# Loading and normalising a small probability table in four parts in place of one

## Chip, cores and metric
The kernel runs on one core of a Trainium2 chip. The metric is the device time of one execution in microseconds (us), median of several runs. The engines are named as in the profile: PE (TensorE), PEld (its weight loads), DVE (VectorE), ACT (ScalarE), POOL (GpSimd), and SP (SyncE), which in this kernel issues all but two of the DMAs, in the order of the program.

## The reference
A linear attention feeds a mixture of four experts. The 2304 tokens of the second stage stand in 18 tiles of 128.

```python
# attention: batch 4, heads 8, sequence 576, head size 64, 128 features
def phi(x):
    proj = np.einsum('bhsd,df->bhsf', x, w_phi)
    proj = proj - np.max(np.abs(proj), axis=-1, keepdims=True)
    return np.concatenate([np.exp(proj), np.exp(-proj)], axis=-1)
q_p, k_p = (phi(q), phi(k))
kv = np.einsum('bhsf,bhsd->bhfd', k_p, v)
num = np.einsum('bhsf,bhfd->bhsd', q_p, kv)
den = np.einsum('bhsf,bhf->bhs', q_p, np.sum(k_p, axis=2))[..., None] + 1e-06
attn_out = num / den
# mixture of experts: x is attn_out as (2304, 512), E = 4, F = 1024
p = domain_probs / (domain_probs.sum(-1, keepdims=True) + 1e-9)
for e in range(E):
    h = np.maximum(x @ w1[e], 0.0)
    out += p[:, e:e + 1] * (h @ w2[e])
```

`domain_probs` is the small table of this case: 2304 rows of 4 numbers of 32 bits.

## The kernel before
The 16 pairs of heads of the attention are worked on one after the other, a new one every 16 "steps" of a clock that exists only while the program is written. Each stage of a pair (load, projection `proj`, its row maxima `m` and the subtraction `d`, exponentials, the product `kv`, the numerator `num`, the denominator's reciprocal `rec`, storing) has a step in a table, and `later(key, fn)` puts it on a heap. `run_until` takes from the heap what is due. From the fourth pair on the experts run in the gaps: `first_units` works through all four experts for the first four token tiles (4 tiles of 128, tiles 0 to 3), and calls `tick()` after every few matmuls, which moves the clock on and issues what is due of the attention. The other 14 tiles follow when the attention is over, in two groups that use Strassen products. So the order of each engine's instructions is set by these keys, and every engine works through its own list in order.

Names that the text uses: `l2` (shown as `l`) is the PSUM tile of an expert's second layer, 128x512. Its pool `ps_l2` has two buffers while the attention runs. DVE frees one by the eviction at line 753, `out = l * pr + out`, which reads the normalised probability `pr` of the tile and expert. `proj` and `num` tiles take turns in `ps_att`, which has three buffers; a `proj` buffer is free when DVE's subtraction at line 333 (`d`) has read it. POOL makes the low parts of numbers that PE multiplies in two pieces: `elo` (line 359), `w1lo` and `w2lo` (line 651), `klo` and `qs` (line 244), each a subtraction of two SBUF tiles. At line 217 DVE casts `qs`, and POOL's subtraction of line 244 on `qs` needs that cast. `mt` and `mb` belong to the query's maxima: `mt` is written to DRAM and read back as a broadcast `mb` (line 297), which DVE subtracts at line 302.

The table is loaded in one DMA at step 38 into `pr` (128 partitions, 18 tiles, 4 experts), and `probs_norm` normalises it at step 46 with four DVE instructions: sums, plus 1e-9, reciprocal, product.

Of the kernel before, what the change touches and what calls it, by code (L numbers as in the profile page):

```python
# [14 lines left out]
ALU = mybir.AluOpType  # L15
AX = mybir.AxisListType
# [4 lines left out]
def kernel(  # L21
# [16 lines left out]
    nc = tc.nc  # L38
    P = 128
# [5 lines left out]
    NE, NFC = w.shape[0], w.shape[1]  # L45
    DM = NP * P
    NTT = NT // P
    NPAIR = B * NP

    N0, N1 = 4, 4  # L50
# [42 lines left out]
    pr = const.tile([P, NTT, NE], F32, name="pr")  # L93
    prs = const.tile([P, NTT], F32, name="prs")
# [22 lines left out]
    def later(key, fn):  # L117
        heapq.heappush(queue, (key, next(count), fn))

    def run_until(key):  # L120
        while queue and queue[0][0] <= key:
            heapq.heappop(queue)[2]()
# [661 lines left out]
    def first_units():  # L784
        pend = []
        for n in range(NU):
            load("w1", n + 2, W_WAIT[0])
            h_hi = hp_.tile([P, 2, 512], F32R, name="h_hi", tag="h_hi")
            h_lo = hp_.tile([P, 2, 512], F32R, name="h_lo", tag="h_lo")
            for f in range(2):  # L790
                for k in range(NP):
                    l1_part(n, f, k)
                    if k < NP - 1:
                        tick()
                ps = banks.pop((n, f))
                nc.scalar.activation(h_hi[:, f], ps, AF.Relu)
                relu_lo(h_lo[:, f], ps, h_hi[:, f])
                tick()
            l1_done(n, W_WAIT[2:])
            if n:  # L800
                load("w2", n + 1, W_WAIT[1])
            for fn in pend:
                fn()
                tick()
            if pend:
                l2_done(n - 1, W_WAIT[2:])
            pend = [
                functools.partial(l2_tile, n, (h_hi, h_lo), j, j, out0[:, j]) for j in range(N0)
            ]
        return pend  # L810
# [8 lines left out]
    def x_load(x, first, nt, wait=0):  # L819
        raw = x.raw = early[0].tile([P, NP, 512], F32, name="xr", tag="xr", bufs=1)  # L820
        a = first * P
        src = xd[:, :, a : a + nt].rearrange("c p t -> p c t")
        after(wait, lambda: nc.sync.dma_start(raw[:, :, :nt], src))
# [49 lines left out]
    def spread(ops, start, gap):  # L873
        for i, fn in enumerate(ops):
            after(start + gap * i, fn)
# [93 lines left out]
    def second_units(pend):  # L969
        xs, ops = xa, None  # L970
        for n in range(NU, 3 * NU):
            hooks = {}
            if n == 2 * NU:
                xs = xb
            if n == 2 * NU - 1:
                ops["t4"] = ops["T1"] + ops["t4"]
                for i, name, start, gap in (
                    (1, "T2", 0.5, 0.5), (2, "t4", 0.5, 1), (4, "T3", 0.5, 1.2),
                    (5, "B22", 0.5, 2.3), (6, "T4", -2, 2.1),
                ):  # L980
                    hooks[i] = functools.partial(spread, ops[name], start, gap)
            if n == 2 * NU - 2:
                ops = x_ops(xb)
                spread(ops["t"] + ops["t3"], 0.4, 1.3)
            if n == NU + 3:
                x_load(xb, xb.first, xb.nt)
                for k in range(NP):
                    after(4 + k, nc.scalar.activation, x0_hi[:, k, : xb.nt], xb.raw[:, k, : xb.nt], AF.Copy)
                    after(
                        6 + k,  # L990
                        lambda k=k: nc.vector.tensor_tensor(
                            x0_lo[:, k, : xb.nt], xb.raw[:, k, : xb.nt],
                            x0_hi[:, k, : xb.nt].bitcast(F32), op=ALU.subtract,
                        ),
                    )
            if n == NU + 6:
                x_load(xb, xb.first + xb.nt // P, xb.nt)
            h = strassen_unit(n, xs, pend, hooks)
            nj = xs.nt // P
            pend = [  # L1000
                functools.partial(
                    l2_tile, n, h[b], j, xs.first + b * nj + j, (out0 if b == 0 else out1[0])[:, j]
                )
                for b in (1, 0) for j in range(nj)
            ]
        for fn in pend:
            fn()
            tick()


    with tc.manual_schedule():
        nc.vector.memset(wbd, 0.0)
        nc.scalar.dma_start(wbd[0:D, 0:NF], w_phi)
        nc.scalar.dma_start(wbd[D:P, NF : 2 * NF], w_phi)
        nc.vector.memset(out0[:, 0, 0:256], 0.0)
        warm = ps_l2.tile([P, 512], F32, name="warm", tag="l2")
        for _ in range(3):
            nc.tensor.matmul(
                warm[:, 0:256], lhsT=out0[:, 0, 0:P], rhs=out0[:, 0, 0:256], start=True, stop=True
            )  # L1020
        run_until(-25)
        make_identity(nc, ident)
        nc.vector.memset(eps, 0.0)
        nc.vector.memset(eps[64:P, 0:1], 1e-6)
        nc.vector.memset(eps[0:64, 1:2], 1e-6)
        for h in range(2):
            r = slice(h * D, (h + 1) * D)
            nc.vector.tensor_copy(wst[r], wbd[r, h * NF : (h + 1) * NF])
        nc.vector.tensor_copy(wst_hi, wst)
        nc.vector.tensor_tensor(wst_lo, wst, wst_hi.bitcast(F32), op=ALU.subtract)  # L1030
        nc.gpsimd.tensor_tensor(wlo0[0:64], wst[0:64], wst_hi[0:64].bitcast(F32), op=ALU.subtract)
        zero = wst_hi[64:P].bitcast(F32)
        nc.gpsimd.tensor_tensor(wlo0[64:P], zero, zero, op=ALU.subtract)
        nc.vector.tensor_copy(wbd_hi, wbd)
        nc.vector.tensor_tensor(wbd_lo, wbd, wbd_hi.bitcast(F32), op=ALU.subtract)
        later(38, lambda: nc.sync.dma_start(pr, probs.rearrange("(t p) e -> p t e", p=P)))

        def probs_norm():
            nc.vector.reduce_sum(prs, pr, axis=AX.X)
            nc.vector.tensor_scalar_add(prs, prs, 1e-9)  # L1040
            nc.vector.reciprocal(prs, prs)
            nc.vector.tensor_tensor(
                pr, pr, prs.unsqueeze(2).to_broadcast([P, NTT, NE]), op=ALU.mult
            )

        later(46, probs_norm)
        for n in range(2):
            for i, kind in enumerate(("w1", "w2")):
                for o, fn in ((0, w_load), (8, w_hi), (11.5, w_lo)):
                    later(FETCH[2 * n + i] + o, functools.partial(fn, kind, n))  # L1050
        run_until(FIRST)
        xa, xb = Pair(), Pair()
        xa.first, xa.nt = N0, 512
        xb.first, xb.nt = N0 + 8, 384
        for x, hi, lo in ((xa, x1_hi, x1_lo), (xb, x0_hi, x0_lo)):
            x.op = {
                "B11": (hi[:, 0:2, : x.nt], lo[:, 0:2, : x.nt]),
                "B21": (hi[:, 2:4, : x.nt], lo[:, 2:4, : x.nt]),
            }
        out1 = []  # L1060

        xa_ops = {}

        def to_early():

            in_stack.close()
            early.append(
                ctx.enter_context(
                    tc.tile_pool(name="early", bufs=1, side="right", reuse_waits="tile")
                )  # L1070
            )
            x_load(xa, xa.first + 4, xa.nt)
            xa_ops.update(x_ops(xa))
            fns = [fn for k in ("t", "T2", "T1", "t3", "T3") for fn in xa_ops[k]]
            for i, fn in enumerate(fns):
                later(LAST_IN + X_IN + X_GAP * i, fn)

        def to_late():

            att_stack.close()  # L1080
            late.append(ctx.enter_context(tc.tile_pool(name="late", bufs=1, reuse_waits="tile")))
            out1.append(late[0].tile([P, 4, DM], F32, name="out1"))

        later(LAST_IN, to_early)
        later(LAST + XA_LATE, to_late)
        clock.key = FIRST
        clock.step = (LAST - FIRST) / (NU * (2 * NP + 2 * N0) * SPREAD)
        pend = first_units()
        clock.key = max(clock.key, LAST + XA_LATE)
        run_until(clock.key)  # L1090
        clock.step = 1
        spread([fn for k in ("B22", "t4", "T4") for fn in xa_ops[k]], XA_START, XA_GAP)
        second_units(pend)
# [38 lines left out]
```

## Time and profile before
| what | value |
|---|---|
| median of 3 runs | 942.47 us (941.11 to 943.03) |
| profiled execution | 941.14 us |
| its span, first to last instruction | 939.0 us |
| PE busy | 930.8 us (99%) |
| DVE busy | 648.1 us (69%) |
| POOL busy | 530.3 us (56%) |
| ACT busy | 439.3 us (47%) |
[...]

The profiled execution is one run; its span leaves out 2.1 us of the device time that the runs count. Shares are averages over stages that differ: the attention ends at about a third of the span, and the four places of this case lie in that third.

### The profile page before, as it was taken

To read this page: it belongs to the slowest core of one execution; us is meant where nothing else is said; L and a number is where in the kernel's file an instruction comes from. 1 tells how busy PE (TensorE), PEld (TensorE's weight loads), DVE (VectorE), ACT (ScalarE), POOL (GpSimd) and SP (SyncE) were. 2 spreads that over 40 slices of the span, in tenths; PEclk is the share of its full clock that TensorE was granted. 3 is DMA by queue.
4 is the path that set the end of the run, shared out by engine and by line. 5 is a ranking of instruction groups with operands and counts; after the bars stand their busy time and mean duration, and the time that the engine had idled before them with its cause. 6 is when DMAs were issued, how large, how long until landed. Compare 5 with 4: busy or idle time off the path is not lost.

```text
span 939.0 us, 13221 instructions
## 1 busy us (share of the span) xinstructions
PE 930.8 (99%) x4834; PEld 810.3 (86%) x4834; DVE 648.1 (69%) x1040; ACT 439.3 (47%) x788; POOL 530.3 (56%) x376
## 2 busy tenths in 40 slices
PE   9999999999999999999999999999999999999998
PEld 8988888888888887888888888888899898989897
DVE  6876888878878689566665555669856565656555
ACT  5676666667666545333333333334524343434331
POOL 5646767757556477544445544444765656565651
PEclk9999999999999999999999999999999999999999
DMA  6644555555653633321211221111151212121201
GB/s 164 147 117 137 149 154 144 148 170 152 170 151 99 193 97 112 88 82 45 79 45 45 71 65 45 45 45 46 45 173 51 91 45 90 45 90 45 90 23 68
DMA packets 77418, 90.70 MB, mean 97 GB/s; under 512 B 38410, under 2 KB 40202, under 8 KB 77354
## 3 DMA queue, kind: packets, MB, share of 16 engines
q1 hardware_dynamic: 77194, 89.80, 32.5%
q8 instruction: 38, 0.62, 0.3%
q14 instruction: 26, 0.21, 0.1%
q10 hardware_dynamic: 160, 0.07, 0.0%
HBM read 81.94 MB, written 7.90 MB: 96 GB/s over the span
## 4 chain that ended last, share of the span: by engine, by line
PE 86%; DMA 6%; DVE 5%; SPq 2%; issue 1%; ACT 1%; POOL 0%; DVEq 0%; ACTq 0%
PE l L743 38%; PE D L949 8%; PE C L949 8%; PE A L949 8%; PE l L779 6%; PE kv L387 4%; PE B L949 4%; PE num L478 3%; PE proj L319 2%; DMA rec_d<-rec 1%; DMA mb<-mt_d 1%; PE proj L253 1%; DMA rb<-rec_d 1%; DVE rb L527 1%; DVE out L753 1%
## 5 line engine op out<-in xcount | busy, mean ns | idle before, releaser
L753 DVE SCALAR_TENSOR_TENSOR out<-l,pr,out 128x512 f32<-128x512 f32 x269 | 200.1, 747 | 119.8 <-PE l L743 118.6
L743 PE MATMUL l<-w2hi,h_lo 128*128 128x512 f32 x574 | 225.3, 392 | 1.0 <-DVE out L753 0.8
L743 PE MATMUL l<-w2hi,h_hi 128*128 128x512 f32 x574 | 224.6, 391 | 0.0
L743 PE MATMUL l<-w2lo,h_hi 128*128 128x512 f32 x574 | 224.4, 391 | 0.0
L651 POOL TENSOR_TENSOR w2lo<-wraw,w2hi 128x1024 fp32r<-128x1024 f32 x48 | 120.0, 2500 | 154.7 <-ACT w2hi L645 86.3
L901 ACT ACTIVATE h_hi<-c 128x512 fp32r<-128x512 f32 (+1 forms) x96 | 53.8, 576 | 187.7 <-DVE c L898 126.2
L743 PEld LDWEIGHTS l<-w2hi,h_lo 128*128 128x128 f32 x574 | 107.9, 188 | 22.7 <-DVE out L753 2.7
L743 PEld LDWEIGHTS l<-w2hi,h_hi 128*128 128x128 f32 x574 | 107.8, 188 | 22.8
L743 PEld LDWEIGHTS l<-w2lo,h_hi 128*128 128x128 f32 x574 | 107.8, 188 | 20.2
L359 POOL TENSOR_TENSOR elo<-e,ehi 128x640 fp32r<-128x640 f32 (+1 forms) x36 | 66.2, 1851 | 47.1 <-ACT ehi L449 44.1
L911 POOL TENSOR_TENSOR c<-u,s 128x512 f32<-128x512 f32 (+1 forms) x32 | 37.6, 1176 | 69.0 <-DVE u L898 65.3
L645 ACT ACTIVATE w2hi<-wraw 128x1024 fp32r<-128x1024 f32 x48 | 50.6, 1054 | 51.3 <-PE l L743 43.5
L908 POOL TENSOR_TENSOR h_lo<-c,h_hi 128x512 fp32r<-128x512 f32 (+1 forms) x32 | 41.9, 1308 | 44.7 <-ACT c L927 44.6
L688 POOL TENSOR_TENSOR w1lo<-wraw,w1hi 128x512 fp32r<-128x512 f32 x64 | 66.3, 1058 | 0.6 <-POOL h_lo L908 0.6
L387 PEld LDWEIGHTS kv<-v,e 128*128 128x128 f32 x512 | 61.8, 192 | 2.4
L688 POOL TENSOR_TENSOR s_lo<-ws,s_hi 128x768 fp32r<-128x768 f32 x32 | 59.4, 1858 | 2.6 <-ACT s_hi L680 2.6
L387 PE MATMUL kv<-v,e 128*128 128x66 f32 x512 | 60.8, 272 | 0.0
L901 ACT ACTIVATE h_hi<-A 128x512 fp32r<-128x512 f32 (+1 forms) x32 | 17.4, 545 | 78.7 <-PE A L949 78.7
L651 POOL TENSOR_TENSOR w1lo<-wraw,w1hi 128x1024 fp32r<-128x1024 f32 x16 | 39.3, 2457 | 24.3 <-ACT w1hi L645 24.3
L779 PE MATMUL l<-x_hi,w1lo 128*128 128x512 f32 x128 | 51.1, 399 | 0.0
L779 PE MATMUL l<-x_hi,w1hi 128*128 128x512 f32 x128 | 50.2, 392 | 0.0
L779 PE MATMUL l<-x_lo,w1hi 128*128 128x512 f32 x128 | 50.1, 391 | 0.0
(185 smaller groups left out, 2152.8 us busy)
## 6 DMA issues: line engine op xcount, KB each, us to landing
wraw<-in_w_dram SPq DMA_DIRECT2D x96, 512.0 KB
kq<-in_kq_dram SPq DMA_DIRECT2D x44, 144.0 KB
mb<-mt_d SPq DMA_DIRECT2D x11, 576.0 KB
kq<-in_kq_dram SPq DMA_DIRECT2D x20, 256.0 KB
rb<-rec_d SPq DMA_DIRECT2D x32, 144.0 KB
out_dram<-out SPq DMA_DIRECT2D x17, 256.0 KB
v<-in_v_dram SPq DMA_DIRECT2D x32, 128.0 KB
xd<-rb SPq DMA_DIRECT2D x8, 256.0 KB
```

Of the source, the lines that this page charges most:

```text
L359: engine.tensor_tensor(lo, e, hi.bitcast(F32), op=ALU.subtract)
L387: nc.tensor.matmul(s.kv[:, to : to + KW], lhsT=e[:, e0 : e0 + NF], rhs=s.v[:, 2 * c + j, h * KW : (h + 1) * KW], start=(c == 0 and j == 0 ...
L645: nc.scalar.activation(hi, raw, AF.Copy)
L651: nc.gpsimd.tensor_tensor(lo, raw, hi.bitcast(F32), op=ALU.subtract)
L688: nc.gpsimd.tensor_tensor(dst, src, hi.bitcast(F32), op=ALU.subtract)
L743: nc.tensor.matmul(ps, lhsT=l[:, f, j * P : (j + 1) * P], rhs=r[:, f, :], start=(f == 0 and k == 0), stop=(f == 1 and k == 2),)
L753: nc.vector.scalar_tensor_tensor(o, ps, p, o, op0=ALU.mult, op1=ALU.add)
L779: nc.tensor.matmul(banks[n, f], lhsT=l[:, ksl], rhs=r[:, k, :], start=(k == 0 and j == 0), stop=(k == NP - 1 and j == 2),)
L901: nc.scalar.activation(h[b][0][:, f, :nt], src, AF.Relu)
L908: nc.gpsimd.tensor_tensor(dst, src, hi.bitcast(F32), op=ALU.subtract)
L911: nc.gpsimd.tensor_tensor(temp("c22"), c["u3"], c["s5"], op=ALU.add)
L949: nc.tensor.matmul(ps, lhsT=l[:, k * P : (k + 1) * P], rhs=r[:, k, :], start=(k == 0 and j == 0 and not again), stop=(k == 1 and j == 2), ...
```

## The change
The load and the normalisation are cut into four parts: token tiles 0 to 3, 4 to 8, 9 to 13 and 14 to 17, loaded at steps 38, 118, 150 and 182, each normalised nine steps after its load (so at step 47 in place of 46 for the first). The instructions are the same four, on 4 or 5 columns in place of 18.

```diff
-        later(38, lambda: nc.sync.dma_start(pr, probs.rearrange("(t p) e -> p t e", p=P)))
-
-        def probs_norm():
-            nc.vector.reduce_sum(prs, pr, axis=AX.X)
-            nc.vector.tensor_scalar_add(prs, prs, 1e-9)
-            nc.vector.reciprocal(prs, prs)
+
+        def probs_load(a, z):
+            src = probs.rearrange("(t p) e -> p t e", p=P)
+            nc.sync.dma_start(pr[:, a:z], src[:, a:z])
+
+        def probs_norm(a, z):
+            part, total = pr[:, a:z], prs[:, a:z]
+            nc.vector.reduce_sum(total, part, axis=AX.X)
+            nc.vector.tensor_scalar_add(total, total, 1e-9)
+            nc.vector.reciprocal(total, total)
             nc.vector.tensor_tensor(
-                pr, pr, prs.unsqueeze(2).to_broadcast([P, NTT, NE]), op=ALU.mult
+                part, part, total.unsqueeze(2).to_broadcast([P, z - a, NE]), op=ALU.mult
             )
 
-        later(46, probs_norm)
+        cuts = ((0, N0, 38), (N0, N0 + 5, 118), (N0 + 5, N0 + 10, 150), (N0 + 10, NTT, 182))
+        for a, z, key in cuts:
+            later(key, functools.partial(probs_load, a, z))
+            later(key + 9, functools.partial(probs_norm, a, z))
```

On PE, ACT and POOL the order of instructions is the same before and after. On DVE the first place is early in the attention, behind the projection of the fourth pair's keys. Before:

```order
L333 TENSOR_TENSOR d<-proj,m 128x512
L1039 TENSOR_REDUCE prs<-pr 128x18
L1040 TENSOR_SCALAR prs<-prs 128x18
L1041 RECIPROCAL prs<-prs 128x18
L1042 TENSOR_TENSOR pr<-pr,prs 128x72
L217 CAST qs<-kq_112 128x512
L508 RECIPROCAL rec<-den 128x9
```

In the changed kernel the same place reads so:

```order
L333 TENSOR_TENSOR d<-proj,m 128x512
L217 CAST qs<-kq_112 128x512
L1043 TENSOR_REDUCE prs<-pr 128x4
L1044 TENSOR_SCALAR prs<-prs 128x4
L1045 RECIPROCAL prs<-prs 128x4
L1046 TENSOR_TENSOR pr<-pr,prs 128x16
L508 RECIPROCAL rec<-den 128x9
```

The cast of `qs` has moved ahead of the four, which have 4 columns in place of 18. The second place on DVE is in the middle of `first_units`, among the evictions of an expert's second layer (the numbers behind `l` tell its tiles apart). Before:

```order
L508 RECIPROCAL rec<-den 128x9
L753 SCALAR_TENSOR_TENSOR out_87<-l_1707,pr,out_87 128x512
L753 SCALAR_TENSOR_TENSOR out_87<-l_1723,pr,out_87 128x512
L331 TENSOR_REDUCE m<-proj 128x4
L333 TENSOR_TENSOR d<-proj,m 128x512
```

In the changed kernel, where the same two tiles are called 1708 and 1728:

```order
L508 RECIPROCAL rec<-den 128x9
L753 SCALAR_TENSOR_TENSOR out_87<-l_1708,pr,out_87 128x512
L1043 TENSOR_REDUCE prs<-pr 128x5
L1044 TENSOR_SCALAR prs<-prs 128x5
L1045 RECIPROCAL prs<-prs 128x5
L1046 TENSOR_TENSOR pr<-pr,prs 128x20
L753 SCALAR_TENSOR_TENSOR out_87<-l_1728,pr,out_87 128x512
L331 TENSOR_REDUCE m<-proj 128x4
L333 TENSOR_TENSOR d<-proj,m 128x512
```

The four new instructions stand between two evictions. The third place on DVE is two pairs later, and there the changed kernel has:

```order
L276 STREAM_TRANSPOSE mxT<-mx_114 128x64
L508 RECIPROCAL rec<-den 128x9
L1043 TENSOR_REDUCE prs<-pr 128x5
L1044 TENSOR_SCALAR prs<-prs 128x5
L1045 RECIPROCAL prs<-prs 128x5
L1046 TENSOR_TENSOR pr<-pr,prs 128x20
L753 SCALAR_TENSOR_TENSOR out_87<-l_2253,pr,out_87 128x512
```

Before, the eviction (of the same tile, then called 2247) followed the reciprocal `rec` at once. The fourth part, two pairs later again, stands likewise behind a reciprocal `rec`, and the row behind it is `m<-proj` of line 331. On SP the new loads of the second and fourth part stand directly behind the store of `mt`, that of the third behind the store of `mt` and a load of weights; in all three cases the broadcast `mb` comes after them, directly or behind a load of weights.

## Rows read from the trace of the kernel before

**Rows 1.** Waits of PE from 85 us on: us in total, times, longest.

```profile
PE l L743 <- DVE out L753: 0.8, 3, 0.5
```

**Rows 2.** Busy time by engine, 40 to 60 and 60 to 80 us, summed.

```profile
sum 40.00, PE 37.77 PEld 33.68 DVE 29.90 ACT 25.45 POOL 22.50; mean PE 18.89 PEld 16.84 DVE 14.95 ACT 12.72 POOL 11.25
```

**Rows 3.** DVE's timeline around the burst: start us, us, instruction, idle before.

```profile
38.07 2.33 DVE L1040 TENSOR_SCALAR prs<-prs 128x18 f32<-128x18 f32 x1
...
40.89 0.42 DVE L217 CAST qs<-kq 128x512 fp32r<-128x512 f32 x1
41.26 0.21 DVE L508 RECIPROCAL rec<-den 128x9 f32<-128x9 f32 x1
```

**Rows 4.** POOL's timeline at the same place.

```profile
37.99 2.38 POOL L651 TENSOR_TENSOR w1lo<-wraw,w1hi 128x1024 fp32r<-128x1024 f32 x1
41.44 1.27 POOL L244 TENSOR_TENSOR qs<-kq,qs 128x512 fp32r<-128x512 f32 x1 [1.07 <-PE proj L319]
```

**Rows 5.** DVE's timeline, an earlier cast.

```profile
12.80 1.31 DVE L217 CAST qs<-kq 128x512 fp32r<-128x512 f32 x1
```

**Rows 6.** POOL's timeline beside that cast.

```profile
12.01 1.81 POOL L244 TENSOR_TENSOR klo<-kq,khi 128x768 fp32r<-128x768 f32 x1
```

**Rows 7.** DVE's timeline where the later bursts will stand, and one pair of subtractions.

```profile
135.76 1.41 DVE L753 SCALAR_TENSOR_TENSOR out<-l,pr,out 128x512 f32<-128x512 f32 x2
...
137.79 0.69 DVE L333 TENSOR_TENSOR d<-proj,m 128x512 f32<-128x512 f32 x1
...
149.63 3.21 DVE L302 TENSOR_TENSOR xT<-xT,mb 128x640 f32<-128x640 f32 x2
...
182.96 0.69 DVE L753 SCALAR_TENSOR_TENSOR out<-l,pr,out 128x512 f32<-128x512 f32 x1
...
184.28 0.69 DVE L333 TENSOR_TENSOR d<-proj,m 128x512 f32<-128x512 f32 x1
...
228.64 0.63 DVE L331 TENSOR_REDUCE m<-proj 128x4 f32<-128x512 f32 x1
229.30 0.69 DVE L333 TENSOR_TENSOR d<-proj,m 128x512 f32<-128x512 f32 x1
```

**Rows 8.** POOL's timeline at those places.

```profile
136.07 2.40 POOL L359 TENSOR_TENSOR elo<-e,ehi 128x1024 fp32r<-128x1024 f32 x1 [2.68 <-ACT ehi L449]
138.43 2.41 POOL L651 TENSOR_TENSOR w1lo<-wraw,w1hi 128x1024 fp32r<-128x1024 f32 x1
...
148.35 1.84 POOL L215 TENSOR_SCALAR khi<-kq 128x640 fp32r<-128x640 f32 x1
150.28 2.02 POOL L244 TENSOR_TENSOR klo<-kq,khi 128x640 fp32r<-128x640 f32 x1
...
181.82 3.95 POOL L359 TENSOR_TENSOR elo<-e,ehi 128x1024 fp32r<-128x1024 f32 x2 [2.27 <-ACT ehi L449]
...
227.47 3.93 POOL L359 TENSOR_TENSOR elo<-e,ehi 128x1024 fp32r<-128x1024 f32 x2 [1.48 <-ACT ehi L449]
```

**Rows 9.** SP's timeline: the table's load, and the place of the third part.

```profile
31.14 0.59 SPq L1036 DMA_DIRECT2D pr<-in_probs_dram  x1
...
164.05 0.41 SPq L637 DMA_DIRECT2D wraw<-in_w_dram  x1
166.25 0.34 SPq L297 DMA_DIRECT2D mb<-mt_d  x1
```

**Rows 10.** PE's timeline behind the first burst.

```profile
44.92 1.34 PE L478 MATMUL num<-e,kvhi 128*128 128x320 f32 x4 [0.20 <-DVE nd L398]
```

**Rows 11.** PE's timeline at the three later places.

```profile
138.87 0.40 PE L743 MATMUL l<-w2hi,h_lo 128*128 128x512 f32 x1
...
139.56 0.28 PE L478 MATMUL num<-ehi,kvlo 128*128 128x256 f32 x1
...
185.81 0.28 PE L478 MATMUL num<-ehi,kvlo 128*128 128x256 f32 x1
...
232.09 0.28 PE L478 MATMUL num<-ehi,kvlo 128*128 128x256 f32 x1
```

## Prediction, made before the changed kernel was run
> **What bounds the kernel now.** I read the page's busy times, then who made TensorE (PE) wait, then the timelines of the engines at the four places where the order of VectorE (DVE) differs. PE is the bound nearly everywhere: from 85 us to the end it waits 0.8 us in all, in three places, each time for a DVE eviction that frees a PSUM buffer [rows 1]. Between 40 and 80 us it is busy for 37.77 us of 40, so idle for 2.23 [rows 2]. So nothing that moves on DVE can bring more than these 2.2 us, but any DVE delay longer than the slack of a PSUM buffer is lost for good, since PE never waits enough later to win it back. The question is how long the small normalisation holds DVE, and what stands behind it.
>
> **What normalisation costs now.** DVE's four instructions come at 37.82 us: sum, add, reciprocal, multiply. The add on 128x18 numbers takes 2.33 us, from 38.07 to 40.40; the reciprocal of 128x9 at 41.26 takes 0.21 [rows 3]. Size does not explain 2.33 us, but GpSimd (POOL) does: it runs a 128x1024 subtraction from 37.99 to 40.37 [rows 4]. DVE's add ends 0.03 us after it. The same shows elsewhere: the cast to qs takes 0.42 us at 40.89 and 1.31 at 12.80 [rows 3, 5], the latter beside a POOL subtraction that runs until 13.82 [rows 6]; the cast ends 0.29 us behind that. Two SBUF-to-SBUF subtractions in a row on DVE at 149.63 take 3.21 us together [rows 7], and POOL has one instruction ending at 150.19 and the next from 150.28 to 152.30 [rows 8]. So a DVE instruction of these kinds waits for POOL's running one to end, then goes first, and the next of DVE waits for POOL's next. It is a turn-taking: two such instructions in a burst can cost two whole POOL instructions. Add and multiply are both of these kinds (one source in SBUF to SBUF; two sources in SBUF). In before, POOL had nothing ready after 40.37 (1.07 us idle [rows 4]), so the multiply went free.
>
> **The change, part by part.** It replaces one load and one burst by four. PE, ACT and POOL keep their order; SP gets three more loads, DVE three more bursts. A small instruction without a wait I take as 0.17 us, an estimate from the 0.21 of the reciprocal, less what neighbours overlap. Without any wait a burst is then some 0.65 us.
>
> Loads. SP's issue of the whole table took 0.59 us [rows 9]. The new ones stand ahead of the broadcast of mt (twice directly, once with a weight load between). SP waits there anyway: the third part stands in front of the issue at 166.25 with the one before it over at 164.46 [rows 9], 1.79 us of idle. I take nothing; the bounds are 0 and 0.59 us for each, should that cover be gone, for a later broadcast delays DVE and so PE's buffers. Every part is loaded some 17 us before its burst, so no burst waits for its load.
>
> First part, 37.8 us. The qs cast now goes ahead of the burst. It gets in before POOL's 1024-wide subtraction, which then ends at about 40.7 in place of 40.37. The add waits for it to 40.75, the reciprocal ends at 40.95. But POOL's next instruction, the qs subtraction, needs that cast; in before it came at 41.44, just after the late cast [rows 4]; now it is ready at 40.75 and runs 1.27 us, to 42.0. The multiply waits for it: 42.15. The reciprocal of 41.26 [rows 3] comes 0.9 us late, and with it the chain that at 44.92 ends PE's 0.20 us wait for DVE [rows 10]. That chain is tight, so +0.9 us. (Were the burst free of waits, the 0.20 would go: the bound on the other side.)
>
> Second part, 136.4 us. The burst stands between two evictions, shown as one row at 135.76 [rows 7]: the second started at 136.4 and ended at 137.17. The sum ends at 136.6; POOL's 1024-wide subtraction runs from 136.07 to 138.47 [rows 8], the add ends at 138.5, the reciprocal at 138.7, and POOL's next, 2.41 us long and ready with no gap [rows 8], holds the multiply to 141.05. The second eviction is 4.65 us late and ends at 141.75. PE's matmul at 138.87 [rows 11] writes the buffer which it frees (there are two): it waits 2.9 us. After 0.69 us of work comes the num matmul of 139.56 [rows 11], in the buffer that the subtraction d at 137.79 reads (a ring of three). That ended at 138.48 and now ends at 143.1, 0.65 us after PE asks. Together +3.5 us. Queued behind the burst is also the reduction mt, on which a broadcast hangs; relative to PE it is 1.1 us later. I price that at nothing, because the subtraction that it feeds, at 149.63, waits for POOL until 150.19 anyway [rows 7, 8]; the bound is 1.1 us.
>
> Third part, 182.96 us. POOL runs two subtractions, 3.95 us from 181.82 [rows 8]; the first, 2.40 long, ends at 184.2, the second at 185.8. Add to 184.25, multiply to 185.95; the eviction of 182.96 is 3.0 us late, and d, which ended at 184.28 + 0.69 = 184.97 [rows 7], ends at 187.97. The num matmul at 185.81 [rows 11] wants its buffer: +2.15 us.
>
> Fourth part, 228.64 us. Again two POOL subtractions, from 227.47 for 3.93 us [rows 8]. Add to 229.9, multiply to 231.55; the reduction of 228.64 is 2.95 us late, d ends at 232.95 in place of 229.99 [rows 7], and PE wants its buffer at 232.09 [rows 11]: +0.85 us.
>
> Sum: 0.9 + 3.5 + 2.15 + 0.85 = 7.4 us. The profiled execution took 941.14 us (span 939.0 and 2.1 around it), so 948.5; the median of the three runs, 942.47, lies 1.33 above it, so 949.9 for the median.
>
> [...] Rows 3 show an add on 18 columns waiting for POOL; none shows one on an odd number of columns, and the second and third part have five. [...] If odd widths were exempt, it is the next rival.
>
> **The rivals.**
> Five-wide adds don't wait (for it: no row has an odd width; against: the multiplies have two SBUF sources as the pair at 149.63 [rows 7] had). Then in the second part only the multiply waits, to 138.6: eviction 2.2 us late, ending at 139.4, PE +0.5, then d to 140.7 against 140.1, +0.6. Third part: 1.4 us late, d at 186.4, +0.6. First and fourth as before: 0.9 + 1.1 + 0.6 + 0.85 = 3.45, so 945.9.
>
> Nothing so small waits (for it: no instruction here is as small; against: 18 columns did). Then each burst is 0.65 us: the eviction of the second part ends at 137.8, ahead of 138.87, d at 139.15 ahead of 139.56; d of the third at 185.6 ahead of 185.81; the fourth has two us. PE loses nothing and wins the 0.20: 942.3.
>
> The other side, faster: the first burst meets no POOL instruction, because POOL's long one at 37.99 is by then not started or done; DVE's chain gets 3 us back and PE's idle 2.2 us up to 80 us [rows 2] go, with the later bursts free as well: 940.3. It decides whether POOL is idle when the add comes at 38.4; in before it was busy then [rows 4].
>
> Worse: at 38.0 POOL's long instruction goes ahead of the cast. Then the cast ends at 40.7, the add waits for the qs subtraction to 42.0 and the multiply for the next one (0.83 us): some 1.85 in place of 0.9; and a load may cost its 0.59 us on SP. 950.9 to 952.5.
>
> **How the numbers follow.** The forecast has 0.58, the five-wide rival 0.12, the one without waits 0.13, faster 0.04, worse 0.13. A measurement of this kernel tells 0.2% (1.9 us) from nothing. Faster by more: 0.04; within: 0.13; slower: 0.58 + 0.12 + 0.13 = 0.83. The range leaves out the two that end at 942.3 and below and the far end of the last: 944.8 to 952.5. Within the forecast alone, with small instructions of 0.1 to 0.25 us and the loads at their bounds, 947.5 to 952.
>
> **What would show it.** Right: adds of 1 to 2.3 us and multiplies of 1.2 to 2.3 us in all four bursts, each ending with a POOL instruction; PE idle near 139 (2.9 and 0.65), 186 and 232 us, named as waits for DVE; the rest of PE as tightly packed as before. Wrong: bursts of 0.6 us, or waits of DVE that PE's order hides because a buffer is asked for later than I read it.

## The result and the profile after
The changed kernel took 951.39 us (median of five executions, 950.65 to 956.46) against 942.47 before: a ratio of 1.0097 with a 95% interval of 1.0073 to 1.0121, so 8.9 us longer. The forecast was 949.9 in a range of 944.8 to 952.5.

The profiled execution is the longest of its five, 956.46 us (span 954.7). The page's busy times stand against the table of before: PE +5.9 us, DVE +9.6, POOL -1.4.

```profile
PE 936.7 (98%) x4834; PEld 813.1 (85%) x4834; DVE 657.7 (69%) x1052; ACT 439.5 (46%) x788; POOL 528.9 (55%) x376
```

The waits of PE from 85 to 340 us (us in total, times, longest) answer to [rows 1]. Behind 340 us there is one of 0.2.

```profile
PE l L743 <- DVE out L753: 3.5, 3, 2.9
PE num L478 <- DVE d L333: 2.4, 2, 1.9
PE proj L319 <- DVE tr L267: 2.0, 2, 1.7
PE proj L253 <- DVE qs L230: 0.4, 1, 0.4
```

In place of 0.8 us PE waits for 8.3. The first two lines hold the waits that were forecast behind the first place. Next the second burst on DVE's timeline (start us, us, instruction), which answers to the first rows of [rows 7].

```profile
142.50 0.69 DVE L753 SCALAR_TENSOR_TENSOR out<-l,pr,out 128x512 f32<-128x512 f32 x1
143.11 0.16 DVE L1043 TENSOR_REDUCE prs<-pr 128x5 f32<-128x20 f32 x1
143.31 2.32 DVE L1044 TENSOR_SCALAR prs<-prs 128x5 f32<-128x5 f32 x1
145.66 0.19 DVE L1045 RECIPROCAL prs<-prs 128x5 f32<-128x5 f32 x1
145.89 2.05 DVE L1046 TENSOR_TENSOR pr<-pr,prs 128x20 f32<-128x20 f32 x1
147.86 0.74 DVE L753 SCALAR_TENSOR_TENSOR out<-l,pr,out 128x512 f32<-128x512 f32 x1
```

POOL's timeline beside the four bursts, which answers to [rows 4] and [rows 8]:

```profile
38.80 2.55 POOL L651 TENSOR_TENSOR w1lo<-wraw,w1hi 128x1024 fp32r<-128x1024 f32 x1
41.31 1.27 POOL L244 TENSOR_TENSOR qs<-kq,qs 128x512 fp32r<-128x512 f32 x1
...
143.20 2.40 POOL L359 TENSOR_TENSOR elo<-e,ehi 128x1024 fp32r<-128x1024 f32 x1 [3.06 <-ACT ehi L449]
145.56 2.34 POOL L651 TENSOR_TENSOR w1lo<-wraw,w1hi 128x1024 fp32r<-128x1024 f32 x1
...
193.79 3.94 POOL L359 TENSOR_TENSOR elo<-e,ehi 128x1024 fp32r<-128x1024 f32 x2 [2.12 <-ACT ehi L449]
...
241.56 3.95 POOL L359 TENSOR_TENSOR elo<-e,ehi 128x1024 fp32r<-128x1024 f32 x2 [1.48 <-ACT ehi L449]
```

At the second burst POOL's first instruction ends at 145.60, the add on five columns at 145.63; POOL's second ends at 147.90, the multiply at 147.94. The sum and the reciprocal, of no larger size, take 0.16 and 0.19 in between. The second eviction starts 5.36 us after the first (147.86 - 142.50); in before it started 0.64 after it (136.4 in the prediction, against 135.76 in [rows 7]). So it is 4.7 us late, where 4.65 was forecast. The adds and multiplies of the other three bursts, on the same engine:

```profile
39.23 2.15 DVE L1044 TENSOR_SCALAR prs<-prs 128x4 f32<-128x4 f32 x1
...
41.63 0.99 DVE L1046 TENSOR_TENSOR pr<-pr,prs 128x16 f32<-128x16 f32 x1
...
195.09 1.15 DVE L1044 TENSOR_SCALAR prs<-prs 128x5 f32<-128x5 f32 x1
...
196.50 1.28 DVE L1046 TENSOR_TENSOR pr<-pr,prs 128x20 f32<-128x20 f32 x1
...
242.87 1.13 DVE L1044 TENSOR_SCALAR prs<-prs 128x4 f32<-128x4 f32 x1
...
244.25 1.29 DVE L1046 TENSOR_TENSOR pr<-pr,prs 128x16 f32<-128x16 f32 x1
```

The first add and multiply end at 41.38 and 42.62, POOL's two instructions at 41.35 and 42.58. The multiplies of the third and the fourth burst end at 197.78 and 245.54, POOL's pairs at 197.73 and 245.51; their adds end at 196.24 and 244.00, the first instructions of POOL's pairs at 196.20 and 243.97. So all eight wait. PE's timeline at the places of [rows 10] and [rows 11] (in brackets the idle time before, and what ended it):

```profile
46.19 1.34 PE L478 MATMUL num<-e,kvhi 128*128 128x320 f32 x4 [0.67 <-DVE nd L398]
...
113.21 0.55 PE L319 MATMUL proj<-wbd_hi,klo 128*128 128x256 f32 x1 [1.72 <-DVE tr L267]
...
148.65 0.50 PE L743 MATMUL l<-w2hi,h_lo 128*128 128x512 f32 x1 [2.86 <-DVE out L753]
...
150.07 0.35 PE L478 MATMUL num<-ehi,kvlo 128*128 128x256 f32 x1 [0.45 <-DVE d L333]
...
199.91 0.35 PE L478 MATMUL num<-ehi,kvlo 128*128 128x256 f32 x1 [1.91 <-DVE d L333]
...
246.55 0.31 PE L478 MATMUL num<-ehi,kvhi 128*128 128x320 f32 x1
247.01 0.36 PE L478 MATMUL num<-ehi,kvlo 128*128 128x256 f32 x1
```

The waits: 0.67 at the first place (0.20 before), 2.86 and 0.45 at the second, 1.91 at the third. At the fourth none is named, but 0.46 us lie between the last two starts, where neighbours of the first kind lie 0.15 apart: 0.31. The wait at 113.21 is at no place of the change; the two repetitions below don't have it. One thing was not forecast at all, and the windows show it (from and to us; length, busy time of each engine with its instructions, then PEclk, DMA share, GB/s):

```profile
112.00:116.00 4.00, 2.79 (x10) 2.53 (x11) 3.90 (x8) 3.36 (x6) 2.08 (x2) 0.62 0.45 110
...
144.00:148.00 4.00, 1.79 (x10) 1.35 (x9) 3.93 (x4) 0.07 (x1) 4.00 (x3) 1.00 0.43 129
148.00:152.00 4.00, 2.90 (x14) 2.45 (x15) 3.93 (x7) 1.15 (x2) 1.41 (x1) 0.81 0.20 67
152.00:156.00 4.00, 4.00 (x19) 3.51 (x19) 2.03 (x4) 2.83 (x5) 0.00 (x0) 0.76 0.37 103
```

PEclk is the granted clock as a share of full speed. It falls at the wait at 113 (0.62) and again behind the one at 148 (0.81), and is at 0.76 from 152 to 156 us, where PE is busy all through (4.00 of 4.00). In before it is 1.00 in the windows from 136 to 148, and 0.999 over the span. Over 148 to 156 us the loss, an estimate from the share that is missing in each window, is 0.19 x 4 + 0.24 x 4 = 1.72 us. Behind the wait of 1.91 us at the third place, by the same view, it stays:

```profile
196.00:200.00 4.00, 2.10 (x12) 1.67 (x12) 3.90 (x7) 0.81 (x2) 4.00 (x3) 1.00 0.38 96
200.00:204.00 4.00, 4.00 (x26) 3.60 (x27) 3.93 (x6) 2.82 (x6) 1.25 (x3) 1.00 0.38 127
```

This execution is not a typical one: its span is 15.7 us above that of before (954.7 against 939.0), where the medians differ by 8.9. The waits at the four places are some 6.0 us of it, the two falls of the clock some 3.4, the wait at 113 us 1.7; the rest is mostly in shorter waits of PE, among them 0.85 us for POOL's `x_lo` near 80 us.

### The profile page after: what moved, and what is told of

It is laid out like the page before. It is cut to its first block, busy times and chain, and to the rows that moved or that the text cites. A ratio compares the mean times of both kernels' runs of the same rounds, so it can differ in the third digit from the quotient of the medians.

```text
span 954.7 us, 13236 instructions
## 1 busy us (share of the span) xinstructions
PE 936.7 (98%) x4834; PEld 813.1 (85%) x4834; DVE 657.7 (69%) x1052; ACT 439.5 (46%) x788; POOL 528.9 (55%) x376
## 4 chain that ended last, share of the span: by engine, by line
PE 78%; DVE 10%; DMA 7%; ACT 2%; SPq 2%; issue 1%; POOL 0%; DVEq 0%; ACTq 0%
PE l L743 36%; PE D L949 8%; PE C L949 8%; PE A L949 8%; PE B L949 4%; PE l L779 4%; PE kv L387 3%; PE num L478 3%; PE proj L319 2%; DMA mb<-mt_d 1%; DVE out L753 1%; DVE rb L527 1%; DVE xT L302 1%; DMA rb<-rec_d 1%; DMA mt_d<-mt 1%
```

## The experiments
**Theory.** The add and the multiply each wait until POOL's running instruction ends; what that costs is what PE asks for next at the place. **Rivals.** The extra loads or their place on SP; the bursts as such, whatever they contain; the smaller sizes. The runs were made in three groups, each on one chip with the kernel before beside it. The first has the changed kernel again, the bursts without the loads, the loads alone and the multiply on POOL (before: 943.73 us); the second the kernel without the add, the first and fourth place alone and the two that move the whole burst (before: 942.28); the third the changed kernel and the bursts without the loads once more, and the two with the first and second place alone (before: 942.83).

**The changed kernel again**, without an edit, in the first and the third group.

> The changed kernel once more, for a second profile beside the runs below. Every theory: 950 to 953 us. In the theory of turn-taking with POOL the four adds take 1.1 to 2.3 us and the four multiplies 1.0 to 2.1 us as in its first profile, each ending with a POOL instruction. PE's waits for DVE at the second part add up to 3 to 4 us, at the third to about 2, at the fourth to about 0.9. If the first profile (956.46 us, the longest of the five runs) holds a chance delay, the PE wait of 1.7 us near 113 us and the fall of the granted clock to 0.6 there are absent.

> The changed kernel once more, for a comparison on one chip with the three other kernels: 8 to 9.5 us above the kernel before, mean clock 0.995 to 0.998.

Measured 952.39, ratio 1.0102 (1.0070 to 1.0135), and 950.05, ratio 1.0091 (1.0058 to 1.0123). PE's wait for the second eviction was 2.6 and 2.05 us, that for d at the third place 2.0 and 2.0. The wait at 113 us is in neither. So the loss comes again each time, and the wait at 113 is no fixed part of it. Three sizes were not as expected: the waits at the second place were to add up to 3 to 4 us and that at the fourth to 0.9 in the first repetition (2.6 and 0.3), and the second repetition was to lie 8 to 9.5 us above before (7.2).

**Bursts without the loads.** The whole table in one load at step 38, the four bursts where they are.

```diff
+        later(38, functools.partial(probs_load, 0, NTT))
         for a, z, key in cuts:
-            later(key, functools.partial(probs_load, a, z))
             later(key + 9, functools.partial(probs_norm, a, z))
```

> The whole table loaded at step 38 as before, the four bursts at steps 47, 127, 159 and 191 as in the change. Turn-taking of DVE with POOL: 949.5 to 953 us, the same as the changed kernel. Loads as the cause (three more DMAs ahead of the broadcast mb): 942 to 944. Both by half: 946 to 948.

> The four bursts on one load, once more, with more executions, beside the changed kernel on the same chip. Theory (the 3 us by which it was shorter than the changed kernel are chance, since the loads alone cost nothing): within 1 us of the changed kernel. Rival (load and burst together cost more than each alone, by the clock): 2 to 4 us shorter than the changed kernel, with a mean clock higher by 0.001 to 0.002.

Measured 949.26 in the first group, ratio 1.0068 (1.0047 to 1.0089), 3.1 us under the changed kernel; in the third group 952.71, ratio 1.0100 (1.0079 to 1.0120), 2.7 us above it. The first lies just under the range of the theory, 949.5 to 953, and far above that of the loads. The sign against the changed kernel turned, so the loads are not the cause, though "within 1 us" was too narrow. The mean granted clock went with the time: 0.9980 over the first five executions, 0.9965 over the six of the second time.

**Loads without the bursts.** The kernel before, with the three later loads added, into a tile that nobody reads.

```diff
+        spare = ip_.tile([P, NTT, NE], F32, name="spare", bufs=1)
+        src = probs.rearrange("(t p) e -> p t e", p=P)
+        for a, z, key in ((N0, N0 + 5, 118), (N0 + 5, N0 + 10, 150), (N0 + 10, NTT, 182)):
+            later(key, lambda a=a, z=z: nc.sync.dma_start(spare[:, a:z], src[:, a:z]))
```

> The kernel before, with its one load and one burst, and three more loads at steps 118, 150 and 182 into a spare tile that nothing reads. Turn-taking: 941.5 to 943.5 us, as before. Loads as the cause: 949 to 952. Both by half: 946 to 948.

Measured 943.77, ratio 1.0007 (0.9991 to 1.0024). Loads alone cost nothing that can be told.

**The multiply on POOL.** Four bursts and loads as changed; the addition of 1e-9 is left out, and POOL multiplies.

```diff
-            nc.vector.tensor_scalar_add(total, total, 1e-9)
             nc.vector.reciprocal(total, total)
-            nc.vector.tensor_tensor(
+            nc.gpsimd.tensor_tensor(
```

> The changed kernel without the addition of 1e-9, which is left out, and with the multiply on POOL in place of DVE; the sums and reciprocals stay on DVE in the same four places, the loads too. Turn-taking: no instruction of a burst on DVE has to wait for POOL, a burst holds DVE for 0.35 us, and the time falls to 941.5 to 944 us (POOL's elo may come up to 1.7 us late behind its multiply). Loads as the cause: 949 to 952. Number of small instructions on DVE as the cause: half of the loss stays, 946 to 948.

Measured 944.58, ratio 1.0007 (0.9989 to 1.0024), 0.6 us above the range that was expected. The multiply takes 0.22 us on POOL, in POOL's own order. DVE's sums and reciprocals stand at the four places of the changed kernel, take 0.11 to 0.16 and 0.18 to 0.19 us, and wait for nobody: at the second place they end at 139.04 and the next eviction starts at 138.95. So what is left of a burst at these places costs nothing that can be told, once none of DVE's instructions has to wait for POOL.

**Without the add.** The changed kernel with the addition of 1e-9 left out; sum, reciprocal and multiply stay on DVE.

```diff
-            nc.vector.tensor_scalar_add(total, total, 1e-9)
```

> This kernel is the changed one without the addition of 1e-9 (left out in all four parts); sum, reciprocal and multiply stay on DVE. Theory (each add and each multiply waits for one POOL instruction to end): now only the multiply waits, for one instruction instead of two. First part: it ends with the 1024-wide POOL subtraction, near 41.4 us, and the chain behind it is not late: 0 to 0.2. Second part: one wait of about 2.2 us, PE loses some 1.1. Third: 0.6. Fourth: 0, since the subtraction d still comes ahead of PE's matmul. Sum 1.7 to 2 us above the kernel before. Rival (what counts is that a burst stands there at all, its instructions and semaphores, not POOL's turns): as in the changed kernel less 0.2 us for each part, 7 to 8 us above. Multiplies of 1.2 to 2.3 us under the theory, each ending with a POOL instruction.

Measured 943.82, ratio 1.0016 (1.0005 to 1.0027), 1.5 us above before, a little under the 1.7 to 2 that the theory had. The second place on DVE and on POOL, two timelines:

```profile
136.79 1.43 DVE L1045 TENSOR_TENSOR pr<-pr,prs 128x20 f32<-128x20 f32 x1
...
138.15 0.74 DVE L753 SCALAR_TENSOR_TENSOR out<-l,pr,out 128x512 f32<-128x512 f32 x1
```

```profile
135.79 2.40 POOL L359 TENSOR_TENSOR elo<-e,ehi 128x1024 fp32r<-128x1024 f32 x1 [2.67 <-ACT ehi L449]
138.15 2.38 POOL L651 TENSOR_TENSOR w1lo<-wraw,w1hi 128x1024 fp32r<-128x1024 f32 x1
```

The multiply ends at 138.22, 0.03 behind POOL's first instruction, and the eviction follows. PE waits for d by 0.45 and 0.42 us at the second and third place; at the first, DVE's reciprocal `rec` starts at 40.44, ahead of the 41.26 of [rows 3]. With one waiting instruction in a burst the loss is 1.5 us, with two it is 5.5 to 9.9: the second wait eats the slack of the buffers and more. The rival by which the bursts as such cost is gone.

**First and fourth place alone.** The other 14 tiles at step 182, and so normalised at 191.

```diff
-        cuts = ((0, N0, 38), (N0, N0 + 5, 118), (N0 + 5, N0 + 10, 150), (N0 + 10, NTT, 182))
+        cuts = ((0, N0, 38), (N0, NTT, 182))
```

> First part as in the changed kernel, the other 14 token tiles loaded at step 182 and normalised at 191 in one burst. Theory (the price of a burst is set by what PE asks for next at its place): 0.6 to 1.2 for the first part with what follows it, 0.9 to 1.1 for the fourth place, so 1.5 to 2.3 us above the kernel before. Rival (every burst costs about the same, some 2 us): 4 to 5 us above. The add and the multiply of the late burst take 1.1 to 1.5 us each although they have 14 columns in place of 4.

Measured 943.20, ratio 1.0006 (0.9994 to 1.0018), so 0.9 us above before. The late burst's add and multiply on DVE, on 14 columns:

```profile
230.22 1.09 DVE L1044 TENSOR_SCALAR prs<-prs 128x14 f32<-128x14 f32 x1
...
231.62 1.27 DVE L1046 TENSOR_TENSOR pr<-pr,prs 128x56 f32<-128x56 f32 x1
```

They are as long as on four columns (1.13 and 1.29), so at this place the size doesn't matter. PE then waits 0.72 us for d. The place sets the price; the two together are somewhat cheaper than the 1.5 that the theory had as its least.

**First and second place alone**, with a load of 14 tiles at step 118, and then with one load for all.

```diff
-        cuts = ((0, N0, 38), (N0, N0 + 5, 118), (N0 + 5, N0 + 10, 150), (N0 + 10, NTT, 182))
+        cuts = ((0, N0, 38), (N0, NTT, 118))
```

```diff
+        later(38, functools.partial(probs_load, 0, NTT))
+        cuts = ((0, N0, 38), (N0, NTT, 118))
         for a, z, key in cuts:
-            later(key, functools.partial(probs_load, a, z))
             later(key + 9, functools.partial(probs_norm, a, z))
```

> First part as in the changed kernel, the other 14 token tiles loaded at step 118 and normalised at 127: of the three later places only the second stays. Theory (that place alone makes PE wait for some 4 to 5 us, and the granted clock falls behind so long a wait): 3.5 us above the kernel before if the clock stays at 1.00, 5 to 6 if it falls, with a mean clock of 0.997 or 0.998 over the span in place of 0.999 to 1.000. Rival (the clock falls because of several waits, or because of the loads, not because of this one): 3 to 3.5 us above and a mean clock of 0.999 to 1.000. Add of 1.5 to 2.4 us and multiply of about 2.05 although they have 14 columns in place of 5.

> The same two bursts, with the whole table in one load at step 38. Theory (loads cost nothing): the time of the kernel with the second load at step 118, within 0.7 us, and the same mean clock. Rival (the load in front of the broadcast of mt moves the burst against POOL's instructions, or lets the clock fall): 1 us or more shorter.

Measured 947.66, ratio 1.0054 (1.0042 to 1.0066), and 948.12, ratio 1.0061 (1.0048 to 1.0075). The two agree within 0.5 us, so again the load plays no part that can be told. They lie 4.8 and 5.3 us above before; together with the run before, the second place alone is worth some 4 to 5 us. The mean clocks are 0.997 and 0.998 in all eleven executions, as the theory had it, but the first time lies below the 5 to 6 us that it gave for that clock. The windows behind the second place, with the load at step 118:

```profile
140.00:144.00 4.00, 1.77 (x11) 1.38 (x10) 3.93 (x5) 0.00 (x0) 4.00 (x3) 1.00 0.39 107
144.00:148.00 4.00, 3.54 (x19) 3.14 (x18) 3.31 (x6) 1.73 (x4) 0.34 (x1) 0.71 0.03 12
148.00:152.00 4.00, 4.00 (x18) 3.37 (x18) 2.62 (x5) 2.79 (x5) 0.00 (x0) 0.86 0.71 209
```

PE is idle for 2.2 us of the first window, and gets 0.71 and 0.86 of the clock in the two after it: 0.29 x 4 + 0.14 x 4 = 1.72 us, as in the changed kernel. The same windows of the four bursts on one load, the first time:

```profile
140.00:144.00 4.00, 1.60 (x8) 0.86 (x6) 3.96 (x5) 0.00 (x0) 3.50 (x2) 1.00 0.25 75
144.00:148.00 4.00, 3.84 (x24) 3.52 (x25) 3.58 (x7) 3.29 (x7) 0.00 (x0) 1.00 0.05 4
```

Here PE is idle for 2.4 us and the clock stays. The second time, by the same view:

```profile
140.00:144.00 4.00, 1.73 (x9) 1.02 (x8) 3.97 (x5) 0.15 (x1) 3.30 (x2) 1.00 0.20 74
144.00:148.00 4.00, 4.00 (x18) 3.80 (x19) 2.25 (x4) 2.45 (x6) 0.00 (x0) 0.57 0.08 7
```

(1 - 0.57) x 4 = 1.72 us once more. Seven profiled executions have add and multiply on DVE at the second place. In six of them the clock fell there, with waits for the eviction of 1.82, 1.98, 2.05, 2.23, 2.62 and 2.86 us; in the seventh, with a wait of 2.11, it did not. At the third place, where five of them have a wait of 1.91 to 2.02 us for d, no fall is seen: the windows of the changed kernel show 1.00, and in three of the others (the second repetition and both times with the bursts on one load) the 128x512 matmuls behind the wait start 0.23 us apart, as in before.

**The whole burst one place later.** The kernel before with its burst at step 47: behind the cast, as the first part, but with 18 columns.

```diff
-        later(46, probs_norm)
+        later(47, probs_norm)
```

> The kernel before with its one burst at step 47 instead of 46, so behind the cast to qs as in the changed kernel, on all 18 columns. Theory (the first part's loss comes from the place behind the cast, by which POOL's next instruction is ready for its turn when the multiply comes): multiply of about 1 us in place of 0.23, PE's wait at 44.9 us grows from 0.2 to 0.7 or 0.9, time 0.5 to 1.3 us above the kernel before. Rival (the first part costs something because of its small size or its shorter load): the time of the kernel before, within 0.3 us.

Measured 942.22, ratio 0.9998 (0.9987 to 1.0010). PE's timeline at the first place:

```profile
45.76 1.34 PE L478 MATMUL num<-e,kvhi 128*128 128x320 f32 x4 [0.71 <-DVE nd L398]
```

The wait is the theory's (0.71, with a multiply of 0.95 us), so it comes from the place and not from the size. The time is the rival's: 0.5 us more of waiting early in the attention isn't seen at the end, though an interval that reaches from 1.2 us under before to 0.9 above it could hide as much.

**The whole burst where DVE has time.** The same at step 59, behind the subtraction d.

```diff
-        later(46, probs_norm)
+        later(59, probs_norm)
```

> The kernel before with its one burst at step 59 instead of 46: behind the subtraction d that ends at 50.8 us, where DVE then has nothing to do for 3.6 us, so that even two waits for POOL end before its next instruction. Theory (a burst costs what it delays on DVE, and the one of before is the cause of PE's 0.2 us wait at 44.9 and of part of the 2.2 us that PE idles between 40 and 80): the wait of 0.2 goes, the time lies 0 to 2 us under the kernel before. Rival (the 2.2 us belong to the transposition and to other chains): no difference, within 0.3 us, and the other waits of PE up to 80 us stay as they are.

Measured 941.46, ratio 0.9986 (0.9973 to 0.9998): 0.2 to 2.5 us less than before (the medians lie 0.8 apart), less than the 0.2% that a single comparison tells, but with an interval that leaves out no change. As one of twelve comparisons it is a hint and not a proof. DVE's timeline:

```profile
49.96 0.18 DVE L1040 TENSOR_SCALAR prs<-prs 128x18 f32<-128x18 f32 x1
50.17 0.27 DVE L1041 RECIPROCAL prs<-prs 128x18 f32<-128x18 f32 x1
50.47 0.23 DVE L1042 TENSOR_TENSOR pr<-pr,prs 128x72 f32<-128x72 f32 x1
54.62 0.21 DVE L508 RECIPROCAL rec<-den 128x9 f32<-128x9 f32 x1 [3.92 <-DMA den<-den_d]
```

The add that takes 2.33 us in [rows 3] takes 0.18 here: POOL is idle from 49.9 to 50.86, and DVE has nothing to do for 3.92 us behind it. The wait of [rows 10] is gone. But PE's idle time between 40 and 80 us, a part of which was to go, is 2.78 us in this execution against 2.23 in [rows 2], so the profile doesn't show where a gain would come from. This version has the shortest median of all, by little.

## Why the prediction was right, step by step
**The mechanism** was right in each burst: adds and multiplies wait for POOL, two per burst, and PE waits where it was forecast. The runs without the add and with the multiply on POOL show it by taking the waits away: 1.5 us and 0.9 us are left of 5.5 to 9.9.

**First part, +0.9.** Too large. The add ended at 41.38 with POOL and the multiply at 42.62 with the qs subtraction, as forecast, but PE's wait grew by 0.47 only (0.67 against 0.20). This execution runs 0.80 us behind that of before at this place (PE's num matmuls without their waits, 46.19 - 0.67 against 44.92 - 0.20), and DVE's reciprocal `rec` starts at 42.54; so it is 0.48 us late, not 0.9. With the burst on 18 columns at the same place the time didn't change at all, within 1.2 us downward and 0.9 upward.

**Second part, +3.5.** The waits were right, 2.86 forecast as 2.9 and 0.45 as 0.65, in the longest execution; in the other profiled ones the first is 1.8 to 2.6. How long it is depends on when the burst meets POOL: its add took 1.24 us where the wait was shortest and 2.32 where it was longest. What the term lacked is the granted clock behind the wait: 1.72 us here, 3.4 in the first repetition and nothing in one of the five.

**Third part, +2.15.** 1.91 in the changed kernel and 2.0 in its repetitions; right.

**Fourth part, +0.85.** 0.31. POOL's pair of subtractions started 4.62 us ahead of PE's matmul in before ([rows 8], [rows 11]) and 5.14 ahead of the time at which it was now due (241.56 against 246.55 + 0.15), so the two waits ended half a microsecond sooner than I reckoned. In the kernel with the first and fourth place alone it was 0.72.

**Loads, 0.** Right: 943.77 against 943.73 with the loads alone. One load in place of several came out 0.5 us longer with two bursts, and with four bursts once 3.1 us shorter and once 2.7 longer.

**The sum** of 7.4 us was near the measured 8.9 in part by luck, because errors cancelled: the first and the fourth term were too large, and the clock was missing. The waits in the profile of the changed kernel are 0.47 + 2.86 + 0.45 + 1.91 + 0.31 = 6.0 us; in the other four profiled executions with the four bursts they add up to 5.0 to 5.4, and the mean of the five is 5.4. The clock makes up the rest: over the 26 executions with the four bursts its mean is 0.9969, over the 66 of before beside them it is 0.9995, and 0.0026 of 950 us is 2.5 us, an estimate. Together 7.9, where the five comparisons of such kernels gave 8.9, 8.7, 7.2, 5.5 and 9.9, a mean of 8.0. The single executions say the same: of the 26 the three with a mean clock of 0.999 or 1.000 lie 3.9 to 6.1 us above the median of before, the eleven with 0.996 or less 6.4 to 17.0. The step that failed is the first one: "any DVE delay longer than the slack of a PSUM buffer is lost for good" counted a wait at its length, and the one at the second place cost more than that in six of seven profiled executions, by an estimated 1.7 to 3.4 us of the clock. Behind that at the third place the clock stayed (1.00 from 196 to 204 us in the changed kernel), so it is counted at its length.

**The rivals.** Five-wide adds do wait: 2.32 and 1.15 us. They end 0.03 and 0.04 us behind POOL's instruction. That an add on an odd width waits as the one on 18 columns does was the author's estimate, on which the terms 3.5 and 2.15 rest; no row of before shows one, and these two adds bear it out. That nothing so small waits fell with the same rows. POOL did have its long instruction running when the first add came, which ended the faster case. The cast got ahead of that instruction, with 0.50 us, so the worse case didn't occur either.

**Open** is why the clock held at the third place and in one execution at the second, with waits as long (1.91 to 2.02 and 2.11 us) as others behind which it fell (1.82 to 2.86); the third place was not run alone. Open is also what delayed the transposition at 113 us in the profiled execution of the changed kernel (with the loads alone PE waited 1.2 us for it, in the other profiled executions with these loads it did not). And PE's wait for `x_lo` near 80 us is named with 0.85 us in the changed kernel, 0.44 in its second repetition and 0.76 with the load at step 118, where the first load is the short one; it is not named in before, nor in three others with the whole table in one load (the burst at step 59, the second run of the four bursts, the first and second place alone). No difference in time that can be told goes with it.

## What to carry to other kernels
Place a small piece of work by what else runs then, not by its size: where POOL was idle the add and the multiply took 0.18 and 0.23 us, beside two long POOL instructions 2.32 and 2.05. Put it where the engine has a pause before its next due instruction (3.92 us at step 59, the shortest median), and prefer one waiting instruction to two in a row (1.5 us of loss here against 5.5 to 9.9). Where PE is the bound, don't take the length of a wait as its full price: look at the granted clock behind it, which here added nothing at one place and, by estimate, 1.7 to 3.4 us in six of seven executions at another.

## What was not expected of the hardware
The granted clock fell at single waits of PE of 1.7 to 2.9 us, though not at all of them: at the third place it held at 1.9 to 2.0. Most falls cost about 1.7 us, estimated as above: 1.72 behind the second place in the windows shown for three kernels, 1.72 and 1.68 there in the second repetition and with the first and second place on one load, and 1.72 from 112 to 120 us in the changed kernel (1.52 of it in the window shown). The longest cost twice that. In the first repetition of the changed kernel one window shows half of the full clock, 0.50, with PE busy all through (4.00 of 4.00), and its two neighbours 0.79 and 0.85 (columns as above):

```profile
140.00:144.00 4.00, 1.38 (x6) 0.91 (x4) 3.93 (x5) 0.00 (x0) 3.71 (x2) 0.79 0.24 76
144.00:148.00 4.00, 4.00 (x18) 3.66 (x17) 2.67 (x5) 1.84 (x4) 0.00 (x0) 0.50 0.01 1
148.00:152.00 4.00, 4.00 (x18) 3.37 (x18) 2.71 (x5) 2.71 (x5) 0.07 (x1) 0.85 0.88 281
```

The loss is by the same estimate 0.21 x 4 + 0.50 x 4 + 0.15 x 4 = 3.4 us, at a wait of 2.62 us, which is not the longest (2.86, with 1.72 behind it). From 152 to 156 us the clock is at 1.00 again. What makes it fall or hold was not shown.

Executions of before seem to have such falls now and then, by their mean clock alone: of 35 beside the second group, 31 had a mean clock of 0.999 or 1.000, and the four with 0.997 or 0.998 averaged 945.1 us against 942.2 for the others.
